# The MLPs of batches 1 and 2 in three blocks of 512 tokens instead of four of 384

## The chip, the cores and the metric

One NeuronCore of a Trainium2 chip runs the whole kernel. The metric is the device time of one execution in microseconds (us), the median of several. TensorE (PE) multiplies matrices into PSUM, VectorE (DVE), ScalarE (ACT) and GpSimd (POOL) work element by element, and SyncE (SP) issues the DMAs. Every engine works off its own instructions in the order in which the program emits them, and waits on semaphores for the others.

## The reference, cut to what matters

Three layers on 4 batches of 768 tokens, 384 channels.

```python
# 1 gated linear attention, 8 heads of 48
f = 1 / (1 + exp(-f_logit))
for t: state = f[t][:, None] * state + outer(k[t], v[t]); y[t] = q[t] @ state
# 2 token mixing of low rank (32), then an MLP with 1536 hidden units
u = x + (x.T @ U @ V).T
x = u + maximum(u @ w_ch1, 0) @ w_ch2
# 3 gated MLP: gelu, layer norm, mixing over tokens with w_sg, w_out
```

## The kernel before

**MLP of layer 2.** All matrices are split into a high and a low fp32r part, and a product is hi·hi + lo·hi + hi·lo. The MLP of a batch is done in two halves of 384 tokens (`mlp`, L561). A half has `KF1` = 12 steps, one for each 128 hidden units. Step f issues 9 matmuls of 384 columns into a PSUM tile `ps_h` (L588, helper L85), the ReLU on ACT into `ah` (L591), its low part `al` on DVE (L592), then the 9 second matmuls of the step before into three banks `ps_ch` (L572), and last `fill`: other work that is put into this step by hand. The last step of a half adds `ps_ch` to `xT` on DVE (L581). I number the steps through: 0 to 23 are batch 0, 24 to 47 batch 1, and so on.

**Inputs of the MLP.** `make_hl` (L158) splits `xT[b]` into `uh` (ACT, L150) and `ul` (POOL, L151). They live in the pool `work` with two buffers.

**Attention of the next batch, in the fill.** While batch b runs its MLP, `plan(b)` (L702) places the attention of batch b+1, in 6 chunks of 128 tokens. A chunk c consists of `a_decay` (ACT sigmoid L351, a DVE scan L367 into one of three tiles `g`, a reciprocal L374, then on POOL the multiplication of k L376 and a small copy L377), `a_grow` (a DVE scan L388 and the multiplication of q L389), `a_scores` (4 transposes of k L403, copied by ACT L405, 16 matmuls q·k into two banks L415, masked by two DVE instructions L423 into `am`), `out_and_load` (`a_out`: the matmuls am·v L445, from chunk 1 on the state T·q L450, then k·v L467; and the loads of the chunk after next but one, L214), `a_state` (DVE, L489 and L491) and `rest` (transposes to `xT` L497, low-rank sums L521). In batches 2 and 3 the scores of chunk c are in step 3c+1 of the 24, decay two and grow one step before, out three steps after, rest six steps after. All of this shares three PSUM banks called `at` by turns.

**Low-rank part.** In steps 22 and 23 of a batch `low_rank_out` (L535) adds the low-rank term to `xT` of the next batch: three matmuls (L541) and three DVE additions (L543) for each half. `make_hl` for the first half follows in step 22.

Within a step, `fill` runs the entries by rank; the order in which they are emitted is each engine's order. After batch 3's MLP, layer 3 runs for all batches.

Of the kernel before, what the change touches and what calls it, by code (L numbers as in the profile page):

```python
# [40 lines left out]
BEGIN = (8, 10, 12, 14, 16, 17)  # L41
UNIT = 384
ALL = slice(None)


def products(l, r):
# [10 lines left out]
def kernel(  # L57
# [79 lines left out]
    def fast(st):  # L137
# [17 lines left out]

        hl = {}

        def make_hl(work, b, hf, part=ALL):  # L158
            if (b, hf) not in hl:
                hl[b, hf] = [work.tile([128, KD, HT], F32R, tag=t, name=t) for t in ("uh", "ul")]  # L160
            hi, lo = hl[b, hf]
            for kd in range(KD)[part]:
                split(hi[:, kd], lo[:, kd], xT[b][:, kd, hf * HT:(hf + 1) * HT])

        w1p = st.enter_context(sp("w1p", 1))
        wp_cm = sp("wp", 1)
# [5 lines left out]

        at_cm = ExitStack()
        cst = at_cm.enter_context(sp("cst", 1, "right"))
        zs = at_cm.enter_context(sp("zs", 4, "right"))
        ld = at_cm.enter_context(sp("ld", 3, "right"))
        aw = at_cm.enter_context(sp("aw", 2, "right"))

        st.enter_context(tc.manual_schedule())
        mask = cst.tile([128, 128], F32, name="mask")  # L180
# [172 lines left out]
        def a_decay(b, c):  # L353
            e = tiles[b, c]
            if "f" not in e:
                a_gate(b, c)
            t, f = e["t"], e["f"]
            n = NP * C
            f3 = f.rearrange("p (h t) -> p h t", h=NP)
            g = gs[(b * NCH + c) % 3]  # L360
# [142 lines left out]
        def low_rank_sum(b, c):  # L503
# [23 lines left out]
                    vec.tensor_tensor(sums[b], h, sums[b], op=ALU.add)  # L527
                    h = sums[b]
            if last:
                hs[b] = aw.tile([128, DM], F32R, tag="hs", name="hs")  # L530
# [4 lines left out]
        def low_rank_out(b, hf, where="at"):  # L535
            for d in range(KD):
                low_rank_add(b, hf, d, where)

        def low_rank_add(b, hf, d, where):
            t = bank(where, [128, HT])  # L540
            pe.matmul(t, lhsT=hs[b][:, d * 128:(d + 1) * 128], rhs=vs[:, hf * HT:(hf + 1) * HT], start=True, stop=True)  # L541
            dst = xT[b][:, d, hf * HT:(hf + 1) * HT]
            vec.tensor_tensor(dst, t, dst, op=ALU.add)  # L543

        def add_ahead(d):
# [2 lines left out]
            return t  # L548

        def hl_from(us):  # L550
            hi = work.tile([128, KD, HT], F32R, tag="uh", name="uh")
            lo = work.tile([128, KD, HT], F32R, tag="ul", name="ul")
# [5 lines left out]

        pend = [lambda: None]

        def mlp(b, hf, fill):  # L561
            u = hl.pop((b, hf))
            ch = []

            def second(f, a):
                if f == 0:
                    ch.extend(bank("ch", [128, HT]) for _ in range(KD))
                last = f == KF1 - 1

                def part(d, i):  # L570
# [6 lines left out]
                for d in range(KD):  # L577
                    part(d, 2)
                    if last:
                        dst = xT[b][:, d, hf * HT:(hf + 1) * HT]  # L580
                        vec.tensor_tensor(dst, ch[d], dst, op=ALU.add)  # L581

            for f in range(KF1):
                hp = bank("h", [128, HT])
                order = [(i, j, kd) for i, j in ((0, 0), (1, 0), (0, 1)) for kd in range(KD)]
                if (b, hf, f) == (0, 0, 0):
                    order.sort(key=lambda x: (x[1], x[2]))
                mm(hp, [(w1s[f][i][:, kd], u[j][:, kd]) for i, j, kd in order])  # L588
                ah = work.tile([128, HT], F32R, tag="ah", name="ah")
                al = work.tile([128, HT], F32R, tag="al", name="al")  # L590
# [4 lines left out]
                fill(hf * KF1 + f)  # L595

        idle = bank("h", [128, 3, 128])

# [84 lines left out]
        def narrow_ahead(f):  # L683
# [13 lines left out]
                pool.tensor_tensor(xT[0][:, f - 5, 0:HT], hi, lo, op=ALU.add)  # L697
            if f in (9, 10):
                for d in range(2 * (f - 9), min(2 * (f - 8), KD)):
                    low_rank_add(0, 1, d, "at")  # L700

        def plan(b):  # L702

            steps = {}

            def put(i, rank, fn, *args):
                steps.setdefault(i, []).append((rank, fn, args))

            if b == 0:
                for f in range(KF1):  # L710
                    put(f, 0, narrow_ahead, f)
                put(KF1 - 4, 8, load, 1, 2)
            put(KF1 // 2 + 1 if b else 10, 9 if b else 1, make_hl, work, b, 1)
            n = b + 1
            for c in range(NCH):
                if b == 0:
                    decay, grow = BEGIN[c], BEGIN[c] + (c > 0)
                    scores, sums, carry, end = [BEGIN[c] + i for i in (2, 3, 4, 4)]
                else:
                    scores = 3 * c + 1  # L720
                    decay, grow, sums, carry, end = scores - 2, scores - 1, scores + 3, scores + 4, scores + 6
                if c + 1 < NCH:
                    put(carry, 1, a_state, n, c)
                else:
                    end = min(end, 2 * KF1 - 3)
                put(grow, 2 if b + c else 4, a_grow, n, c)
                if decay >= 0:
                    put(decay, 3, a_decay, n, c)
                put(end, 4, rest, n, c)
                put(sums, 6 if b else 5, out_and_load, n, c)  # L730
                put(scores, 5 if b else 6, a_scores, n, c)
            if n + 1 < B:
                put(2 * KF1 - 1, 3, a_decay, n + 1, 0)
            put(2 * KF1 - 2, 7, low_rank_out, b + 1, 0)
            put(2 * KF1 - 2, 8, make_hl, work, b + 1, 0)
            put(2 * KF1 - 1, 7, low_rank_out, b + 1, 1)
            return steps

        for b in range(B - 1):
            steps = plan(b)  # L740

            def fill(i):
                for _, fn, args in sorted(steps.get(i, []), key=lambda x: x[0]):
                    fn(*args)
            for hf in range(2):
                mlp(b, hf, fill)
        at_cm.close()

        p2 = ExitStack()
        wn = p2.enter_context(sp("wn", 1, "right"))  # L750
        work2 = p2.enter_context(sp("work2", 2, "right"))
# [32 lines left out]
                nc.sync.dma_start(here[i], w_sg[:, s * S:(s + 1) * S])  # L784

        def side_steps():
            uh, ul = [work.tile([128, KD, HT], F32R, tag=t, name=t) for t in ("uh", "ul")]
# [39 lines left out]
        def fill_last(i):  # L827
# [12 lines left out]
            if i == 3:  # L840
                worst()
            if i == KF1 // 2:
                make_hl(work, B - 1, 1)
            if i < 2 * KD:
                make_hl(work2, 0, i // KD, slice(i % KD, i % KD + 1))

        vec.tensor_reduce(low, gmin.rearrange("p a b -> p (a b)"), axis=AX.X, op=ALU.min)
        fetch_last(0)
        fetch_last(1)
        for hf in range(2):  # L850
            mlp(B - 1, hf, fill_last)
        pend.pop()()
        work_cm.__exit__(None, None, None)
        wp_cm.__exit__(None, None, None)

# [110 lines left out]
        def g_stage(b):  # L966
# [10 lines left out]

            if b + 1 < B:
                for hf, k in enumerate((2, 4) if b else (8, 9)):
                    at(n + k, make_hl, work2, b + 1, hf)  # L980
# [266 lines left out]
```

## Time and profile before

| | us |
|---|---|
| median of 3 runs | 672.09 (672.05 to 672.75) |
| the profiled execution | 674.96 |
| span of its trace | 672.6 |
| mean granted TensorE clock | 0.997 of full speed |
| PE, DVE, ACT, POOL busy | 662.6, 469.8, 277.3, 339.3 |

The span runs from the first to the last instruction; the 2.4 us of the execution outside it are start and end. Busy times of engines overlap. PE's busy time says little of its pace, since matmuls are pipelined and the trace gives each its full latency: what counts is the distance from start to start.

### The profile page before, as it was taken

The page shows a single profiled execution, that of the slowest core. Times are in us where ns is not written, and L with a number is a line of the kernel's source. Part 1 is how long each engine was busy: PE and PEld are TensorE (multiplying, and loading weights), DVE is VectorE, ACT ScalarE, POOL GpSimd, SP SyncE. Part 2 cuts the span into 40 slices and gives each one's busy share as a digit, 9 for nine tenths or more (in the row PEclk, how much of TensorE's full clock was granted, in tenths as well). Part 3 has the DMA queues.
Part 4 walks back from the last instruction along what each step waited for, and adds up shares of the span by engine and source line. Part 5 has one row for each costly group of instructions (what it writes and reads, how often), then busy time and mean ns, then how long its engine had stood idle before and what let it go on. Part 6 is the DMA issues. An engine that isn't in the chain of part 4 may idle for free.

```text
span 672.6 us, 13091 instructions
## 1 busy us (share of the span) xinstructions
PE 662.6 (99%) x5081; PEld 632.3 (94%) x5081; DVE 469.8 (70%) x788; ACT 277.3 (41%) x588; POOL 339.3 (50%) x404
## 2 busy tenths in 40 slices
PE   8999999999999999999999999999999999999996
PEld 5889999999999999999999999899889999989996
DVE  8988876564575255576249865587988998897663
ACT  4787433233322232322225543365248155343611
POOL 6789722131332131332026656389579559758731
PEclk9999999999999999999999999999999999999998
DMA  8991112311111301110014468409404911761252
GB/s 307 396 396 53 60 61 88 98 52 59 59 60 60 104 16 55 63 61 1 2 28 137 118 189 316 153 2 326 166 2 162 360 42 72 253 239 59 91 203 76
DMA packets 36358, 84.89 MB, mean 126 GB/s; under 512 B 4160, under 2 KB 12992, under 8 KB 36288
## 3 DMA queue, kind: packets, MB, share of 16 engines
q1 hardware_dynamic: 36288, 83.97, 35.5%
q8 instruction: 42, 0.69, 0.4%
q14 instruction: 28, 0.23, 0.1%
HBM read 70.98 MB, written 12.98 MB: 125 GB/s over the span
## 4 chain that ended last, share of the span: by engine, by line
PE 81%; DVE 10%; ACT 2%; POOL 2%; DMA 2%; issue 1%; SPq 0%; ACTq 0%; DVEq 0%; POOLq 0%
PE ps_h L85 26%; PE ps_ch L572 18%; PE ps_ch L85 11%; PE ps_at L85 11%; PE ps_at L415 4%; PE ps_at L445 3%; PE ps_at L450 2%; DVE sum L975 1%; POOL w L308 1%; DVE z L107 1%; DVE z L104 1%; PE ps_at L521 1%; PE ps_at L403 1%; PE ps_at L497 1%; PE ps_at L467 1%
## 5 line engine op out<-in xcount | busy, mean ns | idle before, releaser
L592 DVE SCALAR_TENSOR_TENSOR al<-ps_h,ah 128x384 fp32r<-128x384 f32 x96 | 53.3, 555 | 99.8 <-ACT ah L591 99.4
L85 PE MATMUL ps_h<-uh,w 128*128 128x384 f32 x576 | 118.6, 340 | 0.0
L572 PE MATMUL ps_ch<-ah,w 128*128 128x384 f32 x576 | 115.3, 334 | 0.0
L85 PEld LDWEIGHTS ps_h<-uh,w 128*128 128x128 f32 x576 | 99.8, 188 | 1.9
L572 PEld LDWEIGHTS ps_ch<-ah,w 128*128 128x128 f32 x576 | 101.2, 188 | 0.0
L591 ACT ACTIVATE ah<-ps_h 128x384 fp32r<-128x384 f32 x96 | 46.8, 488 | 123.3 <-PE ps_h L85 123.2
L151 POOL TENSOR_TENSOR xl<-x,xh 128x384 fp32r<-128x384 f32 x18 | 18.2, 1011 | 116.3 <-ACT xh L150 96.9
L572 PE MATMUL ps_ch<-al,w 128*128 128x384 f32 x288 | 65.8, 336 | 0.2 <-DVE al L592 0.2
L85 PE MATMUL ps_h<-ul,w 128*128 128x384 f32 x288 | 65.4, 334 | 0.0
L151 POOL TENSOR_TENSOR ul<-xT,uh 128x384 fp32r<-128x384 f32 x45 | 48.8, 1110 | 32.1 <-ACT uh L150 32.1
L151 POOL TENSOR_TENSOR n<-t,n 128x512 fp32r<-128x512 f32 (+1 forms) x48 | 54.9, 1171 | 0.0
L572 PEld LDWEIGHTS ps_ch<-al,w 128*128 128x128 f32 x288 | 51.2, 188 | 0.8 <-DVE al L592 0.8
L85 PEld LDWEIGHTS ps_h<-ul,w 128*128 128x128 f32 x288 | 51.5, 188 | 0.2
L423 DVE TENSOR_TENSOR am<-ps_at,mask 128x512 f32<-128x512 f32 x42 | 27.2, 685 | 25.6 <-PE ps_at L415 25.4
L150 ACT ACTIVATE n<-t 128x512 fp32r<-128x512 f32 (+1 forms) x48 | 27.5, 575 | 37.8 <-DVE t L131 33.6
L151 POOL TENSOR_TENSOR gt<-sum,gt 128x384 fp32r<-128x384 f32 x24 | 25.4, 1067 | 21.6 <-ACT gt L150 21.6
L85 PE MATMUL ps_at<-side,n 128*128 128x384 f32 x189 | 36.2, 336 | 0.0
L85 PE MATMUL ps_ch<-side,n 128*128 128x384 f32 x189 | 36.2, 336 | 0.0
L372 POOL TENSOR_TENSOR fall<-g,fqk 112x4 f32<-112x4 f32 x15 | 3.1, 208 | 61.3 <-DVE g L367 61.3
L85 PEld LDWEIGHTS ps_at<-side,n 128*128 128x128 f32 x189 | 33.1, 188 | 0.0
L85 PEld LDWEIGHTS ps_ch<-side,n 128*128 128x128 f32 x189 | 33.1, 188 | 0.0
L376 POOL TENSOR_TENSOR fqk<-fqk,g 112x512 f32<-112x512 f32 x21 | 27.1, 1291 | 2.7 <-DMA fqk<-in_fqk_dram 2.7
(261 smaller groups left out, 1522.2 us busy)
## 6 DMA issues: line engine op xcount, KB each, us to landing
side<-side SPq DMA_DIRECT2D x87, 384.0 KB, 5.2
fqk<-in_fqk_dram SPq DMA_DIRECT2D x36, 384.0 KB, 3.7
raw<-in_w_dram SPq DMA_DIRECT2D x24, 384.0 KB, 7.9
out_dram<-xT SPq DMA_DIRECT2D x24, 192.0 KB, 2.0
v<-in_v_dram SPq DMA_DIRECT2D x21, 192.0 KB, 3.8
raw<-in_w_in_dram SPq DMA_DIRECT2D x8, 384.0 KB, 3.2
xT<-in_fqk_dram SPq DMA_DIRECT2D x6, 384.0 KB, 5.8
raw<-in_w_sg_dram SPq DMA_DIRECT2D x6, 384.0 KB, 3.8
```

What stands on the lines that cost most here:

```text
L85: pe.matmul(ps, lhsT=l, rhs=r, start=(i == 0), stop=(i == n - 1))
L104: vec.scalar_tensor_tensor(zi, zi, 3, low, op0=ALU.logical_shift_left, op1=ALU.bitwise_or)
L150: act.activation(hi, src, ACTF.Copy)
L151: eng.tensor_tensor(lo, src, hi.bitcast(F32), op=ALU.subtract)
L376: pool.tensor_tensor(k, k, g.rearrange("p h t -> p (h t)"), op=ALU.mult)
L415: pe.matmul(sc[j][:, p, :], lhsT=e["k"][rows, p, :], rhs=e["q"][rows, p, :], start=True, stop=True)
L423: vec.tensor_tensor(am, sc[j], m3, op=ALU.mult)
L445: pe.matmul(y[t, h * D:(h + 1) * D], lhsT=e["am"][h % 2][:, h // 2, t], rhs=vv[:, h * D:(h + 1) * D], start=(h == 0), stop=(c == 0 and h = ...
L450: pe.matmul(y[t, p * 2 * D:(p + 1) * 2 * D], lhsT=e["q"][:, p, t], rhs=T[:, p, :], start=False, stop=(p == NP - 1))
L572: pe.matmul(ch[d], lhsT=w, rhs=a[i // 2], start=(f == 0 and i == 0), stop=(last and i == 2))
L591: act.activation(ah, hp, ACTF.Relu)
L592: vec.scalar_tensor_tensor(al, hp, 0.0, ah.bitcast(F32), op0=ALU.max, op1=ALU.subtract)
```

## The change

The four half MLPs of batches 1 and 2 become three blocks of 512 tokens: "first" (batch 1, tokens 0 to 511), "both" (batch 1's last 256 and batch 2's first 256) and "second" (batch 2, tokens 256 to 767). They are steps 24 to 35, 36 to 47 and 48 to 59. Since "both" needs batch 2, the whole attention of batch 2 is put into the 12 steps of "first": scores of chunk c at step 24 + `MEET[c]`, out at `MEET[c+1]`, rest at `MEET[c+2]`. Batch 3's attention is spread over "both" and "second" as before over a batch. `uh` and `ul` get pools of their own, opened and closed by hand (`u0`, `u1`, `wide0`, `wide1`, `u2`, `u3`); `ah` and `al` are 512 wide; the tiles `g` become two instead of three, `hs` one instead of two.

```diff
+WIDE = 512
+MEET = (0, 1, 2, 4, 5, 7, 8, 9)
...
+        pieces = {(b, hf): [(b, hf * HT, HT, 0)] for b in range(B) for hf in range(2)}
+        pieces["first"] = [(1, 0, WIDE, 0)]
+        pieces["both"] = [(1, WIDE, S - WIDE, 0), (2, 0, S - WIDE, S - WIDE)]
+        pieces["second"] = [(2, S - WIDE, WIDE, 0)]
...
-        gs = [cst.tile([PR, NP, C], F32, name=f"g{i}") for i in range(3)]
+        gs = [cst.tile([PR, NP, C], F32, name=f"g{i}") for i in range(2)]
...
-        def mlp(b, hf, fill):
-            u = hl.pop((b, hf))
+        def mlp(key, fill, base):
+            u = hl.pop(key)
+            n = width(key)
...
-                        dst = xT[b][:, d, hf * HT:(hf + 1) * HT]
-                        vec.tensor_tensor(dst, ch[d], dst, op=ALU.add)
+                        for b, i, w, o in pieces[key]:
+                            dst = xT[b][:, d, i:i + w]
+                            vec.tensor_tensor(dst, ch[d][:, o:o + w], dst, op=ALU.add)
...
-                hp = bank("h", [128, HT])
+                hp = bank("h", [128, n])
...
+        middle, late = 2 * KF1, 3 * KF1
...
+        put(middle - 2, 7, low_rank_out, 1, 0, WIDE)
+        put(middle - 2, 8, make_u, "wide0", "first")
+        put(middle - 1, 7, low_rank_out, 1, WIDE, S)
+        put(middle, 0, swap_left, "u1", "wide1")
+        put(middle + 3, 8, make_u, "wide1", "both", ALL, slice(0, 1))
+        for n, base, meet in ((2, middle, MEET), (3, late, [3 * c + 1 for c in range(NCH + 1)] + [2 * KF1 - 3])):
             for c in range(NCH):
...
+                one, then, end = [base + i for i in meet[c:c + 3]]
+                put(one - 2, 9 if one < base + 2 else 3, a_decay, n, c)
+                put(one - 1, 9 if one < base + 1 else 2, a_grow, n, c)
+                put(one, 5, a_scores, n, c)
+                put(then, 6, out_and_load, n, c)
                 if c + 1 < NCH:
-                    put(carry, 1, a_state, n, c)
...
+                    put(then + 1, 1, a_state, n, c)
                 put(end, 4, rest, n, c)
...
+        put(late - 2, 7, low_rank_out, 2, 0, S - WIDE)
+        put(late - 2, 8, make_u, "wide1", "both", ALL, slice(1, 2))
+        put(late - 1, 7, low_rank_out, 2, S - WIDE, S)
+        put(late + 7, 9, make_u, "wide0", "second")
...
+        for i, key in enumerate(((0, 0), (0, 1), "first", "both", "second")):
+            mlp(key, fill, i * KF1)
```

## Rows read from the trace of the kernel before

**Rows 1.** The page, busy time of the engines, share of the span, instructions.

```profile
PE 662.6 (99%) x5081; PEld 632.3 (94%) x5081; DVE 469.8 (70%) x788; ACT 277.3 (41%) x588; POOL 339.3 (50%) x404
```

**Rows 2.** A stretch of batch 1's MLP: length, then PE, PEld, DVE, ACT, POOL busy, clock, DMA share, GB/s.

```profile
152.50:203.70 51.20, 51.20 (x472) 50.03 (x471) 30.82 (x49) 15.23 (x32) 14.27 (x18) 1.00 0.18 59
```

**Rows 3.** Chain of waits: start, length, what; nine matmuls of a step.

```profile
152.50 1.79 PE ps_h L85 x9
...
155.85 1.56 PE ps_h L85 x9
```

**Rows 4.** Timeline of PE in layer 3: start, length, instruction; 512 columns.

```profile
426.92 0.39 PE L85 MATMUL ps_at<-winh,uh 128*128 128x512 f32 x1
...
428.96 0.39 PE L85 MATMUL ps_h<-winh,uh 128*128 128x512 f32 x1
```

**Rows 5.** Timeline of PE around the start of batch 2's attention.

```profile
140.38 0.68 PE L541 MATMUL ps_at<-vs,hs 128*128 128x384 f32 x3
...
150.87 0.55 PE L403 MATMUL ps_at<-ident,fqk 112*128 112x112 f32 x4
151.34 1.16 PE L415 MATMUL ps_at<-fqk 48*128 48x128 f32 x16
152.43 1.34 PE L85 MATMUL ps_h<-uh,w 128*128 128x384 f32 x6
...
163.50 1.14 PE L445 MATMUL ps_at<-v,am 128*64 128x48 f32 x32
164.47 0.53 PE L467 MATMUL ps_at<-v,kt 128*48 128x48 f32 x16
```

**Rows 6.** Timeline of DVE, the same stretch.

```profile
140.75 1.49 DVE L543 TENSOR_TENSOR xT<-ps_at,xT 128x384 f32<-128x384 f32 x3 [0.65 <-PE ps_at L541]
...
143.79 1.24 DVE L367 TENSOR_TENSOR_SCAN g<-fqk,gone 112x511 f32<-112x511 f32 x1
145.06 0.18 DVE L374 RECIPROCAL fone<-g 112x4 f32<-112x4 f32 x1
...
148.99 1.22 DVE L388 TENSOR_TENSOR_SCAN fqk<-fqk,fone 112x512 f32<-112x512 f32 x1
150.24 0.69 DVE L389 TENSOR_TENSOR fqk<-fqk 112x512 f32<-112x512 f32 x1
150.85 0.55 DVE L592 SCALAR_TENSOR_TENSOR al<-ps_h,ah 128x384 fp32r<-128x384 f32 x1
152.53 1.29 DVE L423 TENSOR_TENSOR am<-ps_at,mask 128x512 f32<-128x512 f32 x2 [1.13 <-PE ps_at L415]
```

**Rows 7.** Timeline of ACT, the same stretch.

```profile
141.35 1.45 ACT L150 ACTIVATE uh<-xT 128x384 fp32r<-128x384 f32 x3 [1.84 <-DVE xT L543]
...
143.14 0.62 ACT L351 ACTIVATE fqk<-fqk 112x512 f32<-112x512 f32 x1
```

**Rows 8.** Groups by line: line, engine, operation, count, busy us, mean ns.

```profile
L150 ACT ACTIVATE n<-t 128x512 fp32r<-128x512 f32 x36 | 22.5, 628 | 25.0 <-DVE t L131 20.8 <-POOL t L943 4.1
L151 POOL TENSOR_TENSOR n<-t,n 128x512 fp32r<-128x512 f32 x36 | 46.5, 1313 | 0.0
L423 DVE TENSOR_TENSOR am<-ps_at,mask 128x512 f32<-128x512 f32 x42 | 27.2, 685 | 25.6 <-PE ps_at L415 25.4
```

**Rows 9.** Timelines of DVE and POOL: a scan that met a POOL multiplication.

```profile
213.60 1.90 DVE L388 TENSOR_TENSOR_SCAN fqk<-fqk,fone 112x512 f32<-112x512 f32 x1
...
213.12 1.30 POOL L376 TENSOR_TENSOR fqk<-fqk,g 112x512 f32<-112x512 f32 x1
```

**Rows 10.** DMA issues: tensor, queue, count, KB each, median us to landing.

```profile
fqk<-in_fqk_dram SPq DMA_DIRECT2D x36, 384.0 KB, 3.7
```

**Rows 11.** A stretch of layer 3, columns as in rows 2.

```profile
500.00:505.00 5.00, 3.54 (x20) 2.90 (x18) 3.61 (x7) 1.63 (x4) 4.61 (x7) 1.00 0.10 38
```

**Rows 12.** Timelines of DVE and POOL at the kernel's start: tiles `g`.

```profile
10.62 1.22 DVE L367 TENSOR_TENSOR_SCAN g<-ps_at,gone 112x511 f32<-112x511 f32 x1
...
8.63 0.18 POOL L377 COPY gmin<-g 112x4 f32<-112x4 f32 x1
```

More of the change, by code (lines that the diff above doesn't have):

```diff
@@ L156, in fast, with width, make_hl @@
         hl = {}
[L158 to L163, printed above, removed]
+        pieces = {(b, hf): [(b, hf * HT, HT, 0)] for b in range(B) for hf in range(2)}
+        pieces["first"] = [(1, 0, WIDE, 0)]
+        pieces["both"] = [(1, WIDE, S - WIDE, 0), (2, 0, S - WIDE, S - WIDE)]
+        pieces["second"] = [(2, S - WIDE, WIDE, 0)]
+        def width(key):
+            return sum(w for _, _, w, _ in pieces[key])
+        def make_hl(pl, key, part=ALL, piece=ALL):
+            if key not in hl:
+                hl[key] = [pl.tile([128, KD, width(key)], F32R, tag=t, name=t) for t in ("uh", "ul")]
+            hi, lo = hl[key]
+            for b, i, w, o in pieces[key][piece]:
+                for kd in range(KD)[part]:
+                    split(hi[:, kd, o:o + w], lo[:, kd, o:o + w], xT[b][:, kd, i:i + w])
         w1p = st.enter_context(sp("w1p", 1))
@@ L174, in fast, with open_u, close_u, make_u @@
         cst = at_cm.enter_context(sp("cst", 1, "right"))
-        zs = at_cm.enter_context(sp("zs", 4, "right"))
         ld = at_cm.enter_context(sp("ld", 3, "right"))
         aw = at_cm.enter_context(sp("aw", 2, "right"))
+        u_pools = {}
+        def open_u(name, *args):
+            cm = sp(name, 1, *args)
+            u_pools[name] = cm, cm.__enter__()
+        def close_u(name):
+            u_pools.pop(name)[0].__exit__(None, None, None)
+        def make_u(name, *args):
+            make_hl(u_pools[name][1], *args)
+        open_u("u0", "right")
+        open_u("u1")
+        zs_cm = sp("zs", 4, "right")
+        zs = zs_cm.__enter__()
         st.enter_context(tc.manual_schedule())
@@ L359, in a_decay @@
             f3 = f.rearrange("p (h t) -> p h t", h=NP)
-            g = gs[(b * NCH + c) % 3]
+            g = gs[(b * NCH + c) % 2]
             def back(a, first, m):
@@ L529, in low_rank_sum @@
             if last:
-                hs[b] = aw.tile([128, DM], F32R, tag="hs", name="hs")
+                hs[b] = aw.tile([128, DM], F32R, tag="hs", name="hs", bufs=1)
                 ends = [act.activation(hs[b], h, ACTF.Copy),
@@ L533, in low_rank_sum, with low_rank_out, low_rank_add @@
                 return ends
-        def low_rank_out(b, hf, where="at"):
+        def low_rank_out(b, lo, hi):
             for d in range(KD):
[L537 to L541, printed above, removed]
-            dst = xT[b][:, d, hf * HT:(hf + 1) * HT]
+                low_rank_add(b, d, lo, hi)
+        def low_rank_add(b, d, lo, hi):
+            t = bank("at", [128, hi - lo])
+            pe.matmul(t, lhsT=hs[b][:, d * 128:(d + 1) * 128], rhs=vs[:, lo:hi], start=True, stop=True)
+            dst = xT[b][:, d, lo:hi]
             vec.tensor_tensor(dst, t, dst, op=ALU.add)
@@ L550, in hl_from @@
         def hl_from(us):
-            hi = work.tile([128, KD, HT], F32R, tag="uh", name="uh")
-            lo = work.tile([128, KD, HT], F32R, tag="ul", name="ul")
+            hi, lo = [u_pools["u0"][1].tile([128, KD, HT], F32R, tag=t, name=t) for t in ("uh", "ul")]
             for d, t in enumerate(us):
@@ L566, in second @@
                 if f == 0:
-                    ch.extend(bank("ch", [128, HT]) for _ in range(KD))
+                    ch.extend(bank("ch", [128, n]) for _ in range(KD))
                 last = f == KF1 - 1
@@ L579, in second @@
                     if last:
-                        dst = xT[b][:, d, hf * HT:(hf + 1) * HT]
-                        vec.tensor_tensor(dst, ch[d], dst, op=ALU.add)
+                        for b, i, w, o in pieces[key]:
+                            dst = xT[b][:, d, i:i + w]
+                            vec.tensor_tensor(dst, ch[d][:, o:o + w], dst, op=ALU.add)
             for f in range(KF1):
-                hp = bank("h", [128, HT])
+                hp = bank("h", [128, n])
                 order = [(i, j, kd) for i, j in ((0, 0), (1, 0), (0, 1)) for kd in range(KD)]
-                if (b, hf, f) == (0, 0, 0):
+                if key == (0, 0) and f == 0:
                     order.sort(key=lambda x: (x[1], x[2]))
                 mm(hp, [(w1s[f][i][:, kd], u[j][:, kd]) for i, j, kd in order])
-                ah = work.tile([128, HT], F32R, tag="ah", name="ah")
-                al = work.tile([128, HT], F32R, tag="al", name="al")
+                ah, al = [work.tile([128, WIDE], F32R, tag=t, name=t)[:, :n] for t in ("ah", "al")]
                 act.activation(ah, hp, ACTF.Relu)
@@ L699, in narrow_ahead @@
                 for d in range(2 * (f - 9), min(2 * (f - 8), KD)):
[L700 to L714, printed above, removed]
-            for c in range(NCH):
[L716 to L721, printed above, removed]
-                if c + 1 < NCH:
-                    put(carry, 1, a_state, n, c)
[L724 to L728, printed above, removed]
-                put(end, 4, rest, n, c)
[L730 to L746, printed above, removed]
+                    low_rank_add(0, d, HT, S)
+        steps = {}
+        def put(i, rank, fn, *args):
+            steps.setdefault(i, []).append((rank, fn, args))
+        def swap_right():
+            zs_cm.__exit__(None, None, None)
+            close_u("u0")
+            open_u("wide0", "right")
@@ new lines, in swap_left @@
+        def swap_left(old, new):
+            close_u(old)
+            open_u(new)
+        middle, late = 2 * KF1, 3 * KF1
+        for f in range(KF1):
+            put(f, 0, narrow_ahead, f)
+        put(KF1 - 4, 8, load, 1, 2)
+        put(10, 1, make_u, "u1", (0, 1))
+        put(KF1 + 1, 0, swap_right)
+        for c in range(NCH):
+            i = BEGIN[c]
+            put(i, 3, a_decay, 1, c)
+            put(i + (c > 0), 2 if c else 4, a_grow, 1, c)
+            put(i + 2, 6, a_scores, 1, c)
+            put(i + 3, 5, out_and_load, 1, c)
+            if c + 1 < NCH:
+                put(i + 4, 1, a_state, 1, c)
+            put(i + 4, 4, rest, 1, c)
@@ new lines, in fast, with fill @@
+        put(late - 2, 7, low_rank_out, 2, 0, S - WIDE)
+        put(late - 2, 8, make_u, "wide1", "both", ALL, slice(1, 2))
+        put(late - 1, 7, low_rank_out, 2, S - WIDE, S)
+        put(late + 7, 9, make_u, "wide0", "second")
+        put(5 * KF1 - 2, 0, swap_left, "wide1", "u2")
+        put(5 * KF1 - 2, 7, low_rank_out, 3, 0, HT)
+        put(5 * KF1 - 2, 8, make_u, "u2", (B - 1, 0))
+        put(5 * KF1 - 1, 7, low_rank_out, 3, HT, S)
+        def fill(i):
+            for _, fn, args in sorted(steps.get(i, []), key=lambda x: x[0]):
+                fn(*args)
@@ L747, in fast @@
+        for i, key in enumerate(((0, 0), (0, 1), "first", "both", "second")):
+            mlp(key, fill, i * KF1)
+        close_u("wide0")
         at_cm.close()
+        open_u("u3")
         p2 = ExitStack()
@@ L786, in side_steps @@
         def side_steps():
-            uh, ul = [work.tile([128, KD, HT], F32R, tag=t, name=t) for t in ("uh", "ul")]
+            uh, ul = [u_pools["u2"][1].tile([128, KD, HT], F32R, tag=t, name=t) for t in ("uh", "ul")]
             places = [[(uh[:, j], 0), (ul[:, j], 1)] for j in range(KD)]
@@ L842, in fill_last @@
             if i == KF1 // 2:
-                make_hl(work, B - 1, 1)
+                make_u("u3", (B - 1, 1))
             if i < 2 * KD:
-                make_hl(work2, 0, i // KD, slice(i % KD, i % KD + 1))
+                make_hl(work2, (0, i // KD), slice(i % KD, i % KD + 1))
         vec.tensor_reduce(low, gmin.rearrange("p a b -> p (a b)"), axis=AX.X, op=ALU.min)
@@ L850, in fast @@
         for hf in range(2):
-            mlp(B - 1, hf, fill_last)
+            mlp((B - 1, hf), fill_last, hf * KF1)
         pend.pop()()
+        close_u("u3")
+        close_u("u2")
         work_cm.__exit__(None, None, None)
```

4 lines of the change are left out of this document (2 added, 2 removed).

## The prediction

> **What bounds the kernel now.** I read the busy times first. PE is busy for 99% of the span [rows 1], so a DVE that is busy for 70% can still be hidden, but nothing that PE does can. Then the windows: in a stretch of batch 1's MLP PE has no gap, DVE is busy for 30.8 of 51.2 us, and the granted clock is 1.00, the upper level of 2.4 GHz [rows 2]. There PE's own pace sets the time. The pace comes from the chain of waits: nine matmuls of 384 columns take 1.56 us, 173.3 ns each from start to start, and 1.79 where attention's small matmuls stood before them [rows 3]. The timeline of layer 3 has the other width: nine of 512 columns take 428.96 - 426.92 = 2.04 us, 226.7 each [rows 4]. The difference of 53.4 ns for 128 columns makes 0.417 ns a column, so 384 columns account for 160 ns and 512 for 213; some 13.4 ns belong to each matmul whatever its width.
>
> **What it removes.** Before, batches 1 and 2 need 4 halves x 12 steps x 18 = 864 matmuls of 384 columns: 864 x 173.3 = 149.7 us. After, 3 x 12 x 18 = 648 of 512: 648 x 226.7 = 146.9. The gain is 2.9 us (0.43%), all of it on the bounding engine. The attention's own matmuls stay, and the steps with attention stay ten for a batch, so their 0.23 us each [rows 3] stay too. The Trainium skill, "TensorE: Matmul & The Clock Gate", section "Wait — 56ns, not 53.3ns?", gives only some 2.5 ns as the fixed cost of a warm matmul; by it the gain would be an estimate of 216 x 2.5 = 0.54 us. The rows give 13.4 and I take them.
>
> **What it moves, and the step that decides.** Batch 2's attention now starts at once: its first two chunks' decay and grow are put into steps 22 and 23, beside the low-rank additions, and its first scores into step 24, not 25. That heaps DVE's work. I follow the clock of the old trace from the first low-rank matmul of step 22, at 140.38 [rows 5].
>
> PE, if it waited for nothing: three low-rank matmuls of 512 0.68, step 23 3.12, three of 256 (120 ns each by the slope) 0.36, so step 24 starts at 144.54. Step 24: 2.04 + 1.56 + transposes 0.47 + scores 1.09 [rows 5] = 5.16. Step 25: 2.04 + 0.23 + 2.04 + 0.47 + 1.09 + out 0.97, and k·v could start at 156.53.
>
> DVE, in its emitted order, from start to start: an addition of 384 takes 0.47 (three in 1.49 [rows 6]); one of 512 from PSUM 0.60 (two masks in 1.29, 0.69 each alone [rows 6, 8]), and by the slope 0.34 at 256; a decay 1.40 (1.27 to the reciprocal and the start of the next); a grow 1.86 (148.99 to 150.85); `al` of 512 0.60, of 384 0.48 [rows 6]. The additions of 512 start at 140.80 and end at 142.69. ACT makes the third `uh` until 143.36 (0.63 each [rows 8], behind each addition as now [rows 7]) and only then batch 2's first sigmoid (0.62 [rows 7]) until 143.95. Then DVE: decay of chunk 0 to 145.4, `al` to 145.9, additions of 256 to 146.9, grow 0 to 148.8, decay 1 to 150.2, `al` of step 24 to 150.8, batch 0's last additions to 152.2, grow 1 to 154.1, decay 2 to 155.5, and the masks of chunk 0 until 156.8. Now the place where PE waits: the transposes and scores of chunk 1 need all three `at` banks, and two of them hold chunk 0's scores until these masks have read them. PE is there at about 154.8 and waits 2.0. After its scores and out the k·v needs a bank that chunk 1's first mask must read; in front of that on DVE are `al` and grow 2 (0.60 + 1.86), which brings it to 159.85. So PE is behind by 159.85 - 156.53 = **3.3 us**.
>
> On top comes POOL. A scan that met POOL's multiplication ended 1.08 after it (213.12 + 1.30 = 214.42, then 215.50) and took 1.90 in place of 1.22 [rows 9]: the two don't run at once. Here decay 0 meets `ul`, whose three parts of 1.31 [rows 8] start at 142.2, and grow 0 meets chunk 0's multiplication of k. If both lose, decay 0 ends at 145.9, the third `ul` at 147.1 (PE wants it at 144.54 + 8 x 0.227 = 146.4), grow 0 at 150.1 in place of 148.8, and the whole tail moves by 1.4: **4.7 us**. Tenths decide who comes first, so I take the middle, 4.0, and keep 3.3 and 4.7.
>
> The masks, out and state of later chunks find DVE idle again: from step 26 on a step has at most one decay, one grow and one state besides `al` (step 27, which has no scores), and the steps with scores last about 8 us on PE (4.1 of MLP and some 4 of attention). I cost them at nothing.
>
> **Smaller edits.** ReLU and `al` at 512 grow by a tenth each, behind 4 us of matmuls: nothing. Six additions of 256 for three of 384 in "both" add 0.6 us to a DVE with room: nothing. Two tiles `g`: the tightest reuse is at the kernel's start, where chunk 2's scan writes at 10.62 the tile whose last POOL reader ended at 8.81 [rows 12]: nothing, down to 1.8 us of room. The own pools: the first write into `wide1` (step 27) is three steps behind the last read of `u1`, `wide0` is free since step 13: nothing. SP's queue: chunks 3 to 5 are loaded at the end of out of chunks 0 to 2 and their decay is one step later, not two or more. The sigmoid waits at the head of ACT for a landing of 3.7 us [rows 10]; in step 29 the nine and nine matmuls of 4.1 us come before PE needs ACT again, so it holds up to a landing of some 5 us; I take nothing, and at worst 2 us where a landing takes 7. A PE that waits might lose its clock: PE was idle for 1.46 of 5 us in one stretch at a granted clock of 1.00 [rows 11], so for waits of 2 us I take nothing; a fall to 1.2 GHz for as long would cost up to 2 us.
>
> **Sum.** -2.9 + 4.0 = +1.1 us. The profiled execution took 674.96 us and would take 676.1. The median of the runs lies 2.87 below the profiled one; the difference goes onto it: 672.09 + 1.1 = **673.2 us**. Bounds of this case: +0.4 to +1.8, 672.5 to 673.9. About 0.2% (1.34 us) is what a measurement of this kernel can tell from no change.
>
> **Rivals.**
> (a) *The start costs nothing.* DVE has 40% free in this stretch [rows 2], and if the early decays find their place ahead of the additions, the masks come in time. Then -2.9: 669.2 us; faster by over 0.2% as long as the waits stay under 1.5. Against it stands that I count 15 us of DVE work in order for 14 us of PE, with the bank rule behind. Chance 0.20.
> (b) *POOL and DVE shut each other out at the next chunks too* (slower). Place: decay 1, grow 1, decay 2, grow 2, each against the multiplication of k of the chunk before. Price 0.68 a meeting [rows 9], all of it ahead of the masks. It decides from 4.2 us of waits on, that is with one meeting beyond the middle; with one beyond 4.7 the waits are 5.4, +2.5: 674.6 us. For it: POOL starts k's multiplication just when DVE turns to the next scan. Against: between them mostly lie `al` or additions, which read PSUM and did not meet POOL in the rows. Chance 0.30.
> (c) *The fixed cost of a matmul is not there in this stage.* If the MLP's matmuls gained only a fifth of the 2.9 us, the gain would be 0.6 and the sum +3.4: 675.5 us. That is what the page's 2.5 ns would make of it. Both paces are read from matmuls that alternate weights like here, so 0.04.
>
> **How the numbers follow.** The forecast has 0.46. Its range lies almost wholly within 0.2%, I give 0.44 to that and 0.02 to slower. So faster 0.20, same 0.44, slower 0.02 + 0.30 + 0.04 = 0.36. The range runs from (a)'s 669.2 to 675.0, which takes in (b) and a little of the late landing; (c) is left out.
>
> **What would show it.** Right: step-to-step distances in batches 1 and 2 of 2.04 for nine matmuls, ps_h and ps_ch both; 648 of them; idle time of PE's weight loads in the first 25 us after step 22, released by DVE's masks L423; DVE without a gap from the low-rank additions to the second chunk's masks. Wrong: a first block without such waits (then (a)), scans of 1.9 beside POOL in it (then (b)), nine matmuls in 2.1 or more, or idle PE in steps 27 to 35, behind a sigmoid that waits for a load.

## The result and the profile after

| | us |
|---|---|
| before, median of 6 runs | 672.31 (672.05 to 672.75) |
| after, median of 6 runs | 678.21 (676.25 to 678.93) |
| ratio, 95% interval | 1.0082 (1.0065 to 1.0098) |
| the profiled execution of after | 678.3, span 676.1 |
| mean granted clock in it | 0.999 |

The change makes the kernel 0.8% slower; I had said 673.2, no difference that can be measured. The 216 matmuls are gone from the page, and PE's share has fallen by a point [rows 1]:

```profile
PE 662.0 (98%) x4865; PEld 603.8 (89%) x4865; DVE 450.7 (67%) x776; ACT 276.1 (41%) x576; POOL 338.7 (50%) x403
```

**The start of the first block.** The timeline of PE, which answers to rows 5 (start, length, instruction, in brackets the idle time and its releaser):

```profile
141.20 0.85 PE L567 MATMUL ps_at<-vs,hs 128*128 128x512 f32 x3
...
147.83 0.50 PE L87 MATMUL ps_h<-ul,w 128*128 128x512 f32 x1 [0.44 <-POOL ul L153]
...
150.88 1.16 PE L441 MATMUL ps_at<-fqk 48*128 48x128 f32 x16 [0.58 <-DVE fqk L415]
...
157.98 1.75 PE L441 MATMUL ps_at<-fqk 48*128 48x128 f32 x16 [1.21 <-DVE am L449]
...
161.63 0.56 PE L493 MATMUL ps_at<-v,kt 128*48 128x48 f32 x16 [0.83 <-DVE am L449]
```

The longest wait is where the prediction put it, at the scores of chunk 1 behind the masks of chunk 0, and the k·v matmuls follow 20.43 us after the first low-rank matmul, in place of the 16.15 that they would need without waits by the prediction's count (156.53 - 140.38): 4.3 us. DVE and POOL in the same stretch, in answer to rows 6 and 9:

```profile
144.73 1.96 DVE L393 TENSOR_TENSOR_SCAN g<-fqk,gone 112x511 f32<-112x511 f32 x1 [1.22 <-ACT fqk L377]
...
148.26 1.84 DVE L414 TENSOR_TENSOR_SCAN fqk<-fqk,fone 112x512 f32<-112x512 f32 x1
...
154.06 1.21 DVE L414 TENSOR_TENSOR_SCAN fqk<-fqk,fone 112x512 f32<-112x512 f32 x1
155.30 0.69 DVE L415 TENSOR_TENSOR fqk<-fqk 112x512 f32<-112x512 f32 x1
155.91 1.22 DVE L393 TENSOR_TENSOR_SCAN g<-fqk,gone 112x511 f32<-112x511 f32 x1
157.16 0.18 DVE L400 RECIPROCAL fone<-g 112x4 f32<-112x4 f32 x1
157.26 1.26 DVE L449 TENSOR_TENSOR am<-ps_at,mask 128x512 f32<-128x512 f32 x2
```

```profile
143.06 4.71 POOL L153 TENSOR_TENSOR ul<-xT,uh 128x512 fp32r<-128x512 f32 x3 [7.33 <-ACT uh L152]
147.73 1.28 POOL L402 TENSOR_TENSOR fqk<-fqk,g 112x512 f32<-112x512 f32 x1
```

DVE has hardly a gap from 144.73 on. Two scans are long, each beside a POOL instruction; those of the next chunks take 1.21 and 1.22.

**The pace.** From the chain of waits (start, length, what), the middle block and then the third one, in answer to rows 3 and 4:

```profile
240.95 2.04 PE ps_h L87 x9
242.99 2.04 PE ps_ch L598 x9
...
307.47 2.08 PE ps_h L87 x9
309.55 2.08 PE ps_ch L598 x9
```

The middle block, "both", has the 2.04 us of rows 4. The first and the third take 2.05 to 2.09 wherever no small matmuls stand before them: something slows two of the three blocks.

**A ledger of the stretch.** For several kernels I added up, from start to start, all that PE does between the first matmul of step 24 and the first matmul behind batch 2's MLP. "Nine" are the MLP's matmuls with what they wait, "rest" is the attention with its waits. With the wide blocks the last nine fall behind this stretch and nine of 384 into it, so 0.48 us (2.04 - 1.56) belong to each of their sums in a comparison with before.

| kernel | nine | rest | sum |
|---|---|---|---|
| before | 151.8 | 53.3 | 205.0 |
| after | 150.5 | 57.3 | 207.7 |
| chunk 0 ahead | 150.3 | 54.3 | 204.5 |
| tiles moved | 149.3 | 57.9 | 207.2 |
| both of these | 149.1 | 54.4 | 203.5 |
| the fastest version | 148.6 | 53.3 | 201.9 |
| scans put into it | 150.6 | 57.0 | 207.6 |

After saves 0.8 us on the nine (151.8 - 150.5 - 0.48) where 2.9 were expected, and pays 4.0 in the rest. The traces of "tiles moved" and "scans put into it" have a lower clock for some microseconds (experiment 6), and their sums contain what it costs.

### The profile page after: what moved, and what is told of

It is laid out like the page before. It is cut to its first block, busy times and chain, and to the rows that moved or that the text cites. A ratio compares the mean times of both kernels' runs of the same rounds, so it can differ in the third digit from the quotient of the medians.

```text
span 676.1 us, 12622 instructions
## 1 busy us (share of the span) xinstructions
PE 662.0 (98%) x4865; PEld 603.8 (89%) x4865; DVE 450.7 (67%) x776; ACT 276.1 (41%) x576; POOL 338.7 (50%) x403
## 4 chain that ended last, share of the span: by engine, by line
PE 77%; DVE 9%; DMA 8%; ACT 2%; issue 1%; POOL 1%; SPq 0%; DVEq 0%; ACTq 0%; POOLq 0%
PE ps_h L87 25%; PE ps_ch L598 16%; PE ps_at L87 13%; PE ps_ch L87 13%; DMA raw<-in_w_dram 3%; PE ps_at L441 3%; PE ps_at L471 3%; DMA fqk<-in_fqk_dram 2%; PE ps_at L476 1%; DVE g L393 1%; DVE z L109 1%; DMA xT<-in_fqk_dram 1%; DVE z L106 1%; DMA side<-side 1%; DVE fqk L414 1%
## 5 line engine op out<-in xcount | busy, mean ns | idle before, releaser
L618 DVE SCALAR_TENSOR_TENSOR al<-ps_h,ah 128x384 fp32r<-128x384 f32 (+1 forms) x84 | 51.4, 612 | 106.2 <-ACT ah L617 106.1
L87 PE MATMUL ps_h<-uh,w 128*128 128x384 f32 (+1 forms) x504 | 116.2, 365 | 0.0
L598 PE MATMUL ps_ch<-ah,w 128*128 128x384 f32 (+1 forms) x504 | 113.4, 360 | 0.0
L598 PEld LDWEIGHTS ps_ch<-ah,w 128*128 128x128 f32 x504 | 91.2, 188 | 9.1
L87 PEld LDWEIGHTS ps_h<-uh,w 128*128 128x128 f32 x504 | 89.2, 188 | 9.6
L617 ACT ACTIVATE ah<-ps_h 128x384 fp32r<-128x384 f32 (+1 forms) x84 | 44.8, 533 | 120.9 <-PE ps_h L87 120.7
L153 POOL TENSOR_TENSOR ul<-xT,uh 128x384 fp32r<-128x384 f32 (+2 forms) x45 | 51.0, 1159 | 37.5 <-ACT uh L152 37.5
L598 PE MATMUL ps_ch<-al,w 128*128 128x384 f32 (+1 forms) x252 | 63.9, 361 | 0.2 <-DVE al L618 0.2
L87 PE MATMUL ps_h<-ul,w 128*128 128x384 f32 (+1 forms) x252 | 63.5, 359 | 0.4 <-POOL ul L153 0.4
L87 PEld LDWEIGHTS ps_h<-ul,w 128*128 128x128 f32 x252 | 46.0, 188 | 5.3 <-POOL ul L153 0.9
```

Of the source, the lines that this page charges most:

```text
L87: pe.matmul(ps, lhsT=l, rhs=r, start=(i == 0), stop=(i == n - 1))
L153: eng.tensor_tensor(lo, src, hi.bitcast(F32), op=ALU.subtract)
L598: pe.matmul(ch[d], lhsT=w, rhs=a[i // 2], start=(f == 0 and i == 0), stop=(last and i == 2))
```

## The experiments

Before's times beside these runs have medians between 672.3 and 672.9. All edits start from the kernel after, but for the one that names before.

**1. The work at the start: one chunk ahead**

```diff
-                put(one - 2, 9 if one < base + 2 else 3, a_decay, n, c)
-                put(one - 1, 9 if one < base + 1 else 2, a_grow, n, c)
+                ahead = 2 if (n, c) == (2, 0) else 0
+                put(one - 2 - ahead, 9 if one < base + 2 else 3, a_decay, n, c)
+                put(one - 1 - ahead, 9 if one < base + 1 else 2, a_grow, n, c)
```

> After, with batch 2's first chunk decayed and grown two steps earlier (steps 20 and 21, beside batch 1's last chunks, where DVE idles 3.8 and 3.4 us at a stretch); all else is as in after. Theory (the loss is at the start of the first 512 block, where the DVE is 19.1 of 21.0 us busy and PE waits for it): 4.6 us of DVE work (scan 1.96, reciprocal, scan 1.84, product 1.03 in after's trace) leaves this stretch, so the 4.3 us that PE loses up to the k-v matmuls of chunk 0 fall to under 1; the time falls by 3 to 4 us, to about 674.5. Rival (PE waits there for the masks of chunks 0 and 1 and for POOL in any case, or the wait only moves to a later chunk): the time falls by under 1 us, to 677.5 or more.

673.6 us (672.87 to 677.33), ratio to before 1.0015 (1.0002 to 1.0028): 4.6 less than after. All that PE still waits in this stretch:

```profile
147.11 0.51 PE L87 MATMUL ps_h<-ul,w 128*128 128x512 f32 x1 [0.22 <-POOL ul L153]
...
157.92 0.56 PE L493 MATMUL ps_at<-v,kt 128*48 128x48 f32 x16 [0.33 <-DVE am L449]
```

So most of the loss at the start is DVE's work for chunk 0. The gain is a little over the 3 to 4 expected. The two traces differ by 3.2 us (207.7 - 204.5 in the ledger), as expected. After's median also holds executions with a lower mean clock, where this run has one in ten; experiment 6 is about that.

**2. The place of the operand tiles**

```diff
+            open_u("pad", "right")
+            u_pools["pad"][1].tile([128, 464], F32, tag="pad", name="pad")
             open_u("wide0", "right")
```

> After, with 1,856 unused bytes above the pool of the first and the third block's uh and ul, which moves these tiles from 864 to 1056 bytes past a multiple of 2,048, where ah, al and the middle block's uh and ul lie; nothing else is changed. Theory (the place of the operand tiles sets the pace of 2.06 to 2.09 us for nine matmuls in the first and third block, against 2.04 in the middle one): the nine take 2.04 in all three blocks outside the steps right behind attention, and the time falls by 1 to 2 us, to about 676.7. Rival (the pace hangs on what the block does, on its waits or on the traffic of the other engines): the nine keep 2.06 to 2.09 in the first and third block, and the time stays at 678.2 within 0.5.

677.23 us (675.46 to 681.79), ratio 1.0071 (1.0042 to 1.01). The same steps of the third block in its chain:

```profile
307.00 2.04 PE ps_h L87 x9
309.04 2.04 PE ps_ch L598 x9
```

The `ps_h` nine take 2.04 in all three blocks outside the steps behind attention; all nine together take 149.3 us against 150.5. The place of the tiles sets the pace. The time fell by 1.0 us, the least that was expected. Two more runs ask what it is about the place: in one all operands move to the offset that seemed bad, in the other the first and third block's go to a third one (208 words of padding).

```diff
+        padl_cm = sp("padl", 1)
+        padl_cm.__enter__().tile([128, 464], F32, tag="padl", name="padl")
         work_cm = sp("work", 2)
```

> After with 1,856 unused bytes below ah and al, which moves ah, al and the middle block's uh and ul from 1056 to 864 bytes past a multiple of 2,048, where the first and the third block's uh and ul lie already. Theory (the pace is 2.04 us for nine where the moving operands of successive matmuls lie at one offset, and 2.06 to 2.09 where the offset changes between uh, ul and ah, al): 2.04 in all three blocks, 1 us less than after. Rival (the offset 1056 by itself is good, 864 bad): 2.06 to 2.09 in all three blocks, 0.5 us more than after.

> After with 832 unused bytes above the pool of the first and third block, so that their uh and ul lie 32 bytes past a multiple of 2,048 and ah, al 1056: 1,024 apart. If what counts is the offset within 2,048 bytes, the nine keep 2.06 to 2.09 us in the first and third block and the time stays at after's 678; if the offset within 1,024 or 512 bytes is enough, 2.04 in all three and 1 us less.

One execution each, 678.46 and 676.16 us, which by itself decides nothing; the pace does. The chain of the first, in the middle block, and of the second, in the third block:

```profile
240.31 2.06 PE ps_h L87 x9
242.37 2.06 PE ps_ch L600 x9
```

```profile
307.05 2.04 PE ps_h L87 x9
309.09 2.04 PE ps_ch L598 x9
```

My theory that the operands must lie at one offset falls twice: with all of them at 864 every block is slow, and with 32 here and 1056 there every block is fast. The offset by itself counts: 32 and 1056 bytes past a multiple of 2,048 give 2.04, 864 gives 2.06, and a mixture of good and bad up to 2.09. Which multiple the chip cares about these three offsets don't tell. No trace shows an address: the offsets are counted from the kernel's pools, and what the runs show are the shifts by 1,856 and 832 bytes.

**3. Both, and the head of the kernel**

> Both edits, the first chunk's decay and growth two steps earlier and the moved uh and ul. If both theories hold, the two gains add, 4 to 6 us off after, to about 673; if only the start counts, 674.5; if neither, 678.

672.3 us (671.86 to 674.99), ratio 1.0002 (0.9991 to 1.0013): the two add up, and the change is worth nothing. The next run is before with `range(2)` and `% 2` for the tiles `g`:

> The kernel before, with two tiles for the decay products in place of three; nothing else is changed. After's trace reaches the nine matmuls of batch 0 at 82.67 us where before's has 81.89. Theory (the third tile that the change gave up is what makes the head of the kernel later): 0.6 to 1.0 us slower than before, 673.1. Rival (the difference between the two traces is one of the load times from run to run): 672.3 within 0.3.

672.68 us (671.98 to 677.33), ratio 1.0006 (0.999 to 1.0021). The interval would leave room for the 0.6 us of the theory, but the trace does not: it reaches the nine matmuls at 81.82 us, before's at 81.89. So the third tile is not the cause. Step 24 starts at 144.57 and 144.53 in the two traces of kernels of before's form, and at 144.6 to 145.4 in the twelve of after's. Of these 0.4 us, 0.1 to 0.2 arise in steps 0 to 23 (103.1 to 103.2 us against 103.0). What makes them was not found.

**4. POOL's part.** `ul` of the first and third block by ACT, then `ul` of the first block set to zero early:

```diff
+                    if key == "first":
+                        act.activation(hi[:, kd, o:o + w], xT[b][:, kd, i:i + w], ACTF.Copy)
+                        act.activation(lo[:, kd, o:o + w], xT[b][:, kd, i:i + w], ACTF.Copy)
```

> After with ul of the first and third block written by ACT, as a plain copy of xT, in place of POOL's subtraction; this leaves the low parts of these two blocks out of the computation and takes POOL's 4.7 us out of the start of the first block. Theory (of the loss at the start, POOL beside DVE's scan makes about 1 us, as the prediction had it with 3.3 without and 4.7 with): DVE's first scan there takes 1.2 us in place of 1.96, the wait for ul (0.44) goes, and the time falls by 0.7 to 1.6 us; the waits for masks stay at 2 us or more. Rival (POOL's presence is the whole of it): the waits at the start fall under 1 us and the time by 3 us or more.

677.1 us (676.59 to 678.94), ratio 1.0061 (1.0046 to 1.0076). Contrary to its text the edit reaches the first block alone (`key == "first"`). DVE's scan takes 1.22, but starts later, since its sigmoid now stands behind ACT's copies, and PE waits 1.35 us at the first scores in place of 0.58:

```profile
150.63 1.16 PE L445 MATMUL ps_at<-fqk 48*128 48x128 f32 x16 [1.35 <-DVE fqk L419]
```

The time is 1.1 us under after's, as the theory had it, but the wait only moved, so the size of POOL's part stays open here. The second try leaves ACT alone:

```diff
+            pool.memset(hl[key][1].bitcast(F32), 0.0)
...
+        put(KF1 + 5, 9, zero_first)
```

> After with ul of the first block set to zero by POOL at step 17, so that POOL has no subtraction at steps 22 to 24; this leaves the low part of the first block's input out of the computation, and ACT's and DVE's work stays as it is. Theory (POOL beside DVE is about 1 us of the loss at the start, as the prediction had it with 3.3 without and 4.7 with): the scan at 144.7 us takes 1.2 in place of 1.96 us, the wait for ul (0.44) goes, and PE's idle time between 147 and 163 us falls from 3.2 to 1.5 to 2.5; the time falls by 0.7 to 1.6 us. Rival (POOL is the whole of it): the idle time falls under 0.7.

676.13 us (675.13 to 677.82), ratio 1.0046 (1.003 to 1.0063). The scan is short, and two of the long waits are left:

```profile
144.48 1.22 DVE L401 TENSOR_TENSOR_SCAN g<-fqk,gone 112x511 f32<-112x511 f32 x1 [1.22 <-ACT fqk L385]
...
156.36 1.75 PE L449 MATMUL ps_at<-fqk 48*128 48x128 f32 x16 [1.22 <-DVE am L457]
...
160.01 0.56 PE L501 MATMUL ps_at<-v,kt 128*48 128x48 f32 x16 [0.83 <-DVE am L457]
```

The idle time falls by 1.0 us to 2.2, as the theory had it, and the stretch of the ledger by 1.4 (207.7 - 206.4). The median falls by more than the 0.7 to 1.6 expected: it is 2.1 us under after's first one and 2.8 under the one in experiment 6, which was taken at the same time. Only one of these six executions has a mean clock under 0.995, which bears on experiment 6. The masks come late without POOL's `ul` too. The Trainium skill, "SBUF — State Buffer", section "SBUF: two separate sides", says that a DVE instruction with two SBUF inputs and a GpSimd one that reads SBUF exclude each other for a whole instruction. The trace agrees as far as it goes: the scan, which reads `fqk` and `gone` in SBUF, takes 1.96 us beside `ul` and 1.22 without it.

**5. A faster version.** With the tiles moved as in 2, chunk 1's decay and growth go ahead as well, and "both" gets its first half of `uh` and `ul` at step 30:

```diff
-        put(middle + 3, 8, make_u, "wide1", "both", ALL, slice(0, 1))
+        put(middle + 6, 8, make_u, "wide1", "both", ALL, slice(0, 1))
...
+                ahead = 2 if n == 2 and c < 2 else 0
```

> After with all that the first runs point to: batch 2's chunks 0 and 1 decayed and grown two steps earlier, the middle block's first half of uh and ul made at step 30 in place of 27, and the 1,856 bytes above the pool of the first and third block. The run with chunk 0 alone ahead and the same 1,856 bytes still shows three PE waits between 140 and 185 us: 0.20 for ul, 0.39 and 0.41 for masks (am) ahead of the k-v matmuls. Theory (both are DVE work beside POOL's k-g products and ul): the two mask waits go, the stretch of the three blocks gets 0.6 to 0.9 us shorter, and the time is 671.4 to 671.8, 0.1 to 0.2% under before. Rival (the waits only move, since DVE now does chunk 1's 4.6 us ahead of the low-rank sums of batch 1): 672.3 or more, no faster than before.

671.8 us (671.39 to 672.38), ratio 0.9986 (0.9977 to 0.9995). Both mask waits are gone, but a new one came, 1.01 us for `ul`: chunk 1's growth in step 22 met POOL:

```profile
148.15 0.50 PE L87 MATMUL ps_h<-ul,w 128*128 128x512 f32 x1 [1.01 <-POOL ul L153]
```

So the growth goes one step later:

```diff
+                if n == 2 and c < 2:
+                    put(base - 4 + c, 9 if c else 3, a_decay, n, c)
+                    put(base - 3 + 2 * c, 9 if c else 2, a_grow, n, c)
```

> As the run with two chunks ahead (671.8), but chunk 1's growth one step later, at step 23 in place of 22, behind batch 1's last low-rank sums. There PE waited 1.01 us for ul, which POOL finished in 5.15 us for three while DVE's scan beside it took 2.01 and its product 1.61. Theory (POOL's ul and DVE's growth hold each other up, and only their meeting has to be avoided): the wait for ul falls to 0.2, no mask wait over 0.2 comes back, and the time is 671.0 to 671.3, 0.2% under before. Rival (the masks of chunk 0 wait for the growth now): a wait of 0.4 us or more at the scores or at the k-v matmuls between 150 and 162 us, and 671.8 or more.

670.81 us (670.33 to 673.19), ratio 0.9964 (0.9951 to 0.9977): 0.36% faster than before beside it, and faster than both kernels. Before's median beside this run is 672.91, a high one; against the 672.31 of the result it is 0.2%. In the traces the stretch is 2.6 us shorter than before's (205.0 - 201.9 - 0.48). PE has no wait left in the stretch:

```profile
146.19 0.86 PE L87 MATMUL ps_h<-ul,w 128*128 128x512 f32 x3
...
148.94 1.16 PE L441 MATMUL ps_at<-fqk 48*128 48x128 f32 x16
...
154.74 1.16 PE L441 MATMUL ps_at<-fqk 48*128 48x128 f32 x16
...
156.80 0.53 PE L493 MATMUL ps_at<-v,kt 128*48 128x48 f32 x16
```

**6. The clock.** The spread of after's times was still open.

> After unchanged, executed some ten times more. In three of the five profiled runs that still have the waits at the start of the first block (2.3 to 3.2 us of PE idle between 150 and 162 us) the granted clock fell to 0.50 right behind them, for 3 to 8 us; in none of the four runs of kernels without them. Theory (a part of after's loss is this clock, and it makes the spread of its times): the times spread from 676 to 679, with a mean clock of 0.995 or less in a third of them and those among the longest; median 677 to 678.5. Rival (the spread is that of the loads and of the last stage): the mean clock is above 0.996 in all, whatever the time.

678.97 us (678.64 to 680.88), ratio 1.0089 (1.0071 to 1.0107), above the 677 to 678.5 of the theory. Five of the six executions have a mean clock of 0.993 or 0.994. With the six first ones that is 7 of 12, and their times are 678.6 to 680.9, against 676.3 for the two fastest at 0.999. But the three others without a low mean take 678.1 to 678.7, so the clock alone does not make the spread. The profiled execution has 0.999 and is long for another reason, a wait in layer 3, which before's trace has too:

```profile
505.57 0.45 PE L87 MATMUL ps_h<-uh,winh 128*128 128x384 f32 x1 [1.44 <-DVE t L944]
```

```profile
501.82 0.44 PE L85 MATMUL ps_h<-uh,winh 128*128 128x384 f32 x1 [1.45 <-DVE t L900]
```

It is behind most of the 2.9 us by which before's profiled execution was above its median [rows 11]: the run with two tiles `g` lacks this wait, and from the end of the stretch its trace takes 320.9 us against before's 323.0. Both kernels have it, so it has nothing to do with the change. For the clock, the fastest version gets waits by another cause:

```diff
+            for _ in range(3):
+                vec.tensor_tensor_scan(to, a, a, 1.0, op0=ALU.mult, op1=ALU.max)
...
+        put(2 * KF1, 4, scans)
```

> The fastest kernel of this study (670.8, no PE wait over 60 ns between 140 and 380 us) with three scans of 464 elements more on DVE in step 24, ahead of the masks of chunk 0, whose result nobody uses: some 3.4 us of DVE work that puts PE's waits at the start of the first block back by another cause. Theory (PE's waits there bring the lower granted clock, whatever DVE is busy with): 2 to 3.4 us of PE waits between 150 and 162 us, and in a third of the executions or more a mean clock of 0.995 or less, these some 2 us above the others; median 673 to 676. Rival (the lower clock of after has another cause, its tile places or the traffic around it): the waits come back, 672.8 to 674.2, and the mean clock stays above 0.996 in all but one of the executions.

676.49 us (676.11 to 676.79), ratio 1.006 (1.0046 to 1.0074): slower than the theory's upper end, though the waits come to 1.9 us and not to 2 or more. All five executions have 0.992 or 0.994. The windows of its trace (length, PE, PEld, DVE, ACT, POOL busy, clock, DMA share, GB/s) and PE's one long wait:

```profile
154.00:156.00 2.00, 1.00 (x7) 0.65 (x5) 1.97 (x3) 0.54 (x1) 0.82 (x1) 1.00 0.03 9
156.00:158.00 2.00, 1.26 (x14) 1.07 (x15) 2.00 (x4) 0.00 (x0) 0.00 (x0) 1.00 0.00 0
158.00:160.00 2.00, 2.00 (x38) 1.88 (x34) 1.97 (x3) 0.00 (x0) 0.00 (x0) 0.62 0.00 0
160.00:162.00 2.00, 1.89 (x22) 1.54 (x21) 0.83 (x2) 1.01 (x2) 0.60 (x1) 0.50 0.00 0
162.00:164.00 2.00, 2.00 (x6) 1.52 (x6) 0.00 (x0) 0.00 (x0) 0.40 (x1) 0.50 0.37 107
164.00:166.00 2.00, 2.00 (x8) 1.59 (x7) 0.03 (x1) 0.66 (x2) 0.00 (x0) 0.68 0.00 0
```

```profile
156.63 1.75 PE L441 MATMUL ps_at<-fqk 48*128 48x128 f32 x16 [1.64 <-DVE am L449]
```

Behind the wait the clock goes to 0.50, the lower level of 1.2 GHz, although PE is busy again, and by these rows it stays there for 6.8 us. Its stretch is 5.6 us longer than the fastest version's (207.55 - 201.94). Its waits of over 60 ns sum to 1.9, and 6.8 us at half the clock cost an estimated 3.4: nearly all of the other 3.7 is the clock. A shorter fall, of 3.4 us by its rows, stands in the trace of the run with the tiles moved, whose waits are after's but for the last (2.4 us in sum):

```profile
156.00:158.00 2.00, 0.74 (x5) 0.36 (x3) 1.97 (x5) 0.54 (x1) 1.24 (x2) 1.00 0.00 0
158.00:160.00 2.00, 1.89 (x23) 1.65 (x24) 1.97 (x4) 0.00 (x0) 0.32 (x2) 0.68 0.00 0
160.00:162.00 2.00, 2.00 (x46) 2.00 (x43) 1.72 (x3) 0.34 (x1) 0.00 (x0) 0.50 0.00 0
162.00:164.00 2.00, 2.00 (x14) 1.60 (x11) 0.00 (x0) 0.68 (x2) 1.01 (x1) 0.96 0.29 90
```

The traces of the third offset and of `ul` by ACT have such a fall too, from 159.1 and 159.9 us on. Both traces of after itself have none, and neither has that of all tiles at 864 nor that without `ul` at the start: the same waits do not always bring it.

The mean clocks tell of the other executions. They are a coarse sign, since the trace of the tiles moved has a fall and a mean of 0.997. Of 35 executions of the seven kernels with a wait of 1.2 us or more at the scores of chunk 1, 19 have 0.995 or less: all five with the scans, 7 of 12 of after, but one of six without `ul` at the start. Of 33 executions of the three versions with one or two chunks ahead and the tiles moved, which have no wait of more than 1.01 us there, none has. Among the rest without such waits it is rare but not absent: one of ten with chunk 0 alone ahead, one of ten with two tiles `g`, one of 70 of before; where the clock fell in these three was not traced. So PE's waits make the lower clock likely. The run with the scans does not tell their DVE work apart from the wait that they cause, but after's waits come without such scans. What decides in a single execution stays open.

## Why the prediction was wrong

**The gain: right.** The stretch of the fastest version has 148.6 us of MLP matmuls against 151.8: 3.2 less, 2.7 after the 0.48. The prediction had 2.9 from 13.4 ns for each matmul. Rival (c), with a gain of 0.6, is refuted. The 2.5 ns of the Trainium skill, "TensorE: Matmul & The Clock Gate", section "Wait — 56ns, not 53.3ns?", made 0.54 us of it; the measurement decides against them for these matmuls.

**The start: right.** Predicted were 3.3 to 4.7 us, middle 4.0, with PE waiting at chunk 1's scores for chunk 0's masks and then at k·v. Measured are 4.3 up to k·v. Both meetings with POOL took place. Rival (a) falls with that, and so does (b) as it was put: the scans of chunks 1 and 2 there take 1.21 and 1.22 us. One meeting came elsewhere, in step 28, where a scan beside POOL took 1.88 and PE waited 0.32.

**The steps that failed were two costed at nothing.** First, "for waits of 2 us I take nothing" for the clock. The row behind it, 1.46 us of idle PE in 5 us at a clock of 1.00 [rows 11], showed one wait that the clock survived; the new waits are 0.44, 0.58, 1.21, 0.11 and 0.83 us within 15. 7 of 12 executions have a mean clock of 0.993 or 0.994, and where a trace shows the fall, it comes right behind waits like these and lasts 3.4 or 6.8 us, an estimated 1.7 to 3.4 us of time. Its share of after's median stays open: the two fastest executions of after are 4.0 us above before, its median 5.9, and not all of these 1.9 us are the clock's, since three executions without a low mean take 678.1 to 678.7. One of these is late for the wait in layer 3; the profiled execution of the result is another, without that wait and with its clock at 1.00 in this stretch. The prediction gave "up to 2 us" as its cost and then left it out of the sum and of the range.

Second, the own pools, also costed at nothing, were looked at for when their tiles come free, not for where they lie. The new place slows two blocks: 1.2 us (150.5 - 149.3, and 150.3 - 149.1 with chunk 0 ahead), close to half of the gain.

**The sum as measured**: -2.7 for the fewer matmuls, +1.2 for their place, +4.4 for the waits (4.0 in the rest, 0.44 for `ul`): 2.9 us, and the two stretches differ by 3.2 (207.7 + 0.48 - 205.0). The two shortest executions are 4.0 above before. The head with some 0.4 is part of what is missing. Another part lies behind the stretch: the eight traces of after's form without a long wait there take 321.6 to 322.2 us to the end of the span, less the 0.48, against 320.9 in the run with two tiles `g`. What makes these differences was not found. The conversion from the profiled execution to the median was right in the main, as the 1.45 us wait in layer 3 shows.

## What to carry to other kernels

Where the busiest engine is PE, a plan that makes it wait at a new place costs the waits and, on top, what the clock loses behind them; here a few of them, none over 1.7 us, were enough in 19 of 35 executions. Before moving work into a stretch, add up the other engines' work in order there, and send ahead what has its data already: two steps earlier was enough here, except that chunk 1's growth could go only one, since it met POOL at two (1.01 us of wait). After a change of layout, compare the pace of the same matmuls block by block, since the address of an operand alone can change it.

## What the runs showed of the hardware

- The place in SBUF of the moving operand changes the pace of 512-column fp32r matmuls: nine in 2.04 us at offsets of 32 and 1056 bytes past a multiple of 2,048, in 2.06 at 864, and up to 2.09 where the two kinds alternate. The offsets are counted from the kernel's pools.
- With the scans put in, PE was busy for 2.3 of 4 us (one wait of 1.64 us among them), and then the granted clock fell to 0.50 with PE busy again; all five executions have a low mean clock. With after's waits, 3.2 us in five pieces, 7 of 12 have one, and the same program runs with either. One wait alone was survived: 1.45 us in layer 3 at a clock of 1.00 [rows 11].
- A DVE scan with two SBUF inputs takes 1.96 us beside POOL's subtraction into `ul` and 1.22 without it.
